# Four prompt-attention layers on one core: when a spare PSUM bank is handed back, how side tiles are spaced in the last layer's first chunk, and how the first weights arrive

## The chip, the cores and the metric

One core of a Trainium2 chip runs the whole kernel in one launch. The metric is the device time of one execution in microseconds. Before the change three runs took 2162.75, 2163.64 and 2164.74 us, median 2163.64. By about 0.2% (4.3 us) and less, two kernels of this length are treated here as equal.

## The reference

`x` is 2048 tokens by 640 features. Four attention layers are applied, each as `x = x + f(layernorm(x))`, in the order A, B, A, B. Both A and B have 32 heads of 20 features; A and B have their own `wqkv` (640 x 1920) and `wo` (640 x 640).

```
qkv = x @ wqkv                       # q, k, v: 32 heads of 20
scores = einsum("bhqd,bhkd->bhqk", q, k) * 20 ** -0.5
A: scores masked to 0 <= row - col < 256     # layers 0 and 2
B: all 2048 x 2048 scores, no mask           # layers 1 and 3
out = softmax(scores) @ v, then @ wo
```

The exponentials of layers 1 and 3 are 2 x 32 x 2048 x 2048 numbers. They decide which engine is busy longest.

## The kernel before, in words

**Tiles.** Scores are made transposed: 128 keys by 512 queries of one head is one *tile*, one PSUM bank. A *unit* (class `Unit`) is one group of four heads (`g`, 0 to 7) of one layer `l` and one chunk `c` of 512 queries. A unit of a full layer has 16 key blocks x 4 heads = 64 tiles; a windowed unit has 12. Layer 1's chunk 0 and layer 3's chunk 0 are cut by keys (`PARTS`): layer 3's chunk 0 into a part of 48 tiles (key blocks 0 to 11) and a part of 16 (blocks 12 to 15) per head group, since keys of the last chunk exist only after layer 2's last chunk.

**The loop.** The list `units` is the order of work; layers are interleaved. After layer 1's last chunk it holds: layer 3 chunk 0 part one for groups 0 to 3, the eight windowed units of layer 2 chunk 3, part one for groups 4 to 7, part two for groups 0 to 7, and then layer 3 chunks 1 to 3 (`index[3, 1, 0, None]` is where those begin). One pass of the main loop is a *tick*: score matmuls (L1427) of two or three tiles into one of two PSUM areas (banks 0 to 2, or 3 to 5 and 6), one exponential on ACT over all of them (L1453), and, a few ticks later, the four matmuls of a key block with the values (L1486) into bank 7.

**Side tiles.** Some tiles of layers 1 and 3 don't go to ACT. `side_giver` picks a loaded unit, `side_take` takes tiles from its end, and VectorE (DVE) makes the exponential: `side_fixed` (L1000) reads the scores out of PSUM, then for each pair of tiles a `chain` of four steps, `fraction` L1016, `square` L1024, `cubic` L1028 and `whole` L1034. In layer 1 a tile may be taken at the earliest `GAP_1` = 5 ticks after the one before and only while the planner's estimate of DVE's backlog, `state["lag"]`, is under `LAG_1` = 0.5; the steps `cubic` and `whole` are cut into two halves of 512 columns, and `side_work` fills DVE up to a backlog of `WORK_1` = 1.4. Once `side["late"]` is set, there is no gap, the limits are `LAG` = 0.95 and `WORK` = 2.2, and the steps are whole (1024 columns). `side_start` sets it when layer 3 chunk 0 part one reaches group 4 and no windowed unit holds `qa` or `ka`. Its buffers are two score buffers, one temporary in `spare`, where layer 2's weights were, and five output buffers in `ka_all` and `qa_all`.

**Background.** Projections (`project`), values (`t_v`), layer norm (`t_ln`), output projections (`t_out`, L600 is its DVE add) and the softmax tails (`t_tail`, `scaled`) are generators. `pump` advances them by the credit that `rate` gives out, so that a task is done some 16 ticks before the unit that needs it. `require` runs what is missing at once, when a unit can't wait. Each background block takes a PSUM bank with `take_m`, is read out by DVE (`evac`, L350, or L600, L1155, L1196) and gives the bank back with `drop_m`. After the interleaved start (`state["early"]` false) the only such bank is number 6: `drop_m` marks it free from the next tick on. TensorE's instructions stand in one queue, so a block that is issued before DVE has emptied bank 6 holds up all scores behind it. `keep_clock` adds dummy matmuls (masks by identity) where the planner finds TensorE too idle; on a tick in which bank 6 isn't free they go in front of the next tick's scores.

**The start.** The weights of layer 0 come on SyncE's queue (L136) into `raw`, a view of `spare`, as four transfers of 320 columns; `get_w` copies 80 columns at a time into padded tiles (POOL L363 zeroes, DVE L365 copies). `first_ln` normalises the first chunk at the same time.

Of the kernel before, what the change touches and what calls it, by code (L numbers as in the profile page):

```python
# [20 lines left out]
D = 640  # L21
# [3 lines left out]
KD = D // P  # L25
G = 8
C = 512
NC = S // C
EPS = 1e-5
SCALE = DH ** -0.5  # L30
HD = D // 2
# [7 lines left out]
KA = 18  # L39
LAG = 0.95  # L40
LAG_1 = 0.5
WORK = 2.2
WORK_1 = 1.4
# [1 line left out]
PRE_1 = 0.8  # L45
KEEP = 30
HALF = True
HALF_3 = False
MOST_1 = 64
GAP_1 = 5  # L50
QA = 4

PARTS = {
    l: [(e[n], e[n + 1]) for n in range(len(e) - 1)]
    for l, e in ((1, (0, 4, 8, 12, 16)), (3, (0, 12, 16)))
}
# [3 lines left out]
def kernel(  # L60
# [10 lines left out]
    nc = tc.nc  # L71
# [29 lines left out]
    spare = big.tile([P, 3 * KD * C], BF16, name="spare", tag="spare")  # L101
    raw = spare[:, 0 : KD * 2 * D].rearrange("p (c f) -> p c f", c=KD)
# [13 lines left out]
    ka_all = big.tile([P, KA, C], BF16, name="ka", tag="ka")  # L116
    kas = [ka_all[:, n, :] for n in range(KA)]
    qa_all = big.tile([P, QA, C], BF16, name="qa", tag="qa")
# [10 lines left out]
    wq_view = [w.rearrange("(c p) f -> p c f", p=P) for w in wqkv_in]  # L129
    nc.sync.dma_start(out=x_sb[:, 0:2, :], in_=xin[:, 0:2, :])  # L130
    nc.sync.dma_start(out=x_sb[:, 2:4, :], in_=xin[:, 2:4, :])

    for h in range(2):
        for n in range(2):
            a = n * D + h * HD
            nc.sync.dma_start(out=raw[:, :, a : a + HD], in_=wq_view[0][:, :, a : a + HD])  # L136
    nc.sync.dma_start(out=wv_sb[0][:], in_=wq_view[0][:, :, 2 * D : 3 * D])
    for c in range(1, NC):
        nc.sync.dma_start(out=x_sb[:, 4 * c : 4 * c + 4, :], in_=xin[:, 4 * c : 4 * c + 4, :])
# [6 lines left out]
    def load_wop(w, dense):  # L146
# [9 lines left out]
        out=ident[:], in_=ident[:], compare_op=ALU.not_equal, fill=1.0,  # L156
# [6 lines left out]
    for m, b, ge in (  # L163
# [6 lines left out]
            out=v, in_=v, compare_op=ALU.is_ge if ge else ALU.is_gt, fill=0.0,  # L170
# [29 lines left out]
    ready = set()  # L200
    todo = []
    tails = []
    state = {"tick": 0, "held": None, "credit": 0.0, "early": True, "act": True, "unit": 0, "heat": 0.0, "carry": 0.0, "least": 0.0, "floor": 0.0, "owed": 0, "lag": 0.0, "want": 0}
# [75 lines left out]
    mfree = {5: (0, 0), 6: (0, 1)}  # L279
    mseq = [1]  # L280
# [9 lines left out]

    def drop_m(b):
        mseq[0] += 1
        mfree[b] = (state["tick"] + (not state["early"]), mseq[0])

    def end_early():
        while mfree[5][0] == 1 << 30:
# [22 lines left out]
    live = Counter()  # L319
# [210 lines left out]
    ka = {}  # L530
    qa = {}
# [233 lines left out]
    early = deque(Unit(1, 0, g, p) for p in PARTS[1][:3] for g in range(G))  # L765
# [17 lines left out]
    index = {(u.l, u.c, u.g, u.part): n for n, u in enumerate(units)}  # L783
# [91 lines left out]
    def finish_unit(u):  # L875
# [33 lines left out]

    side_out = {}  # L910
    side = {
        "xi": deque(), "chain": deque(), "out": deque(), "late": False, "early": False,
        "half": None, "at": 0, "last": 0,
    }
    givers = [u for u in units if not u.windowed and (u.l, u.c) != (1, 0)]
# [1 line left out]
    def side_tiles(xi, t, outs):  # L917

        side["xi"].extend(xi)
        side["t"] = t  # L920
        side["out"].extend(outs)

    def side_start():

        assert not side["chain"] and side["half"] is None
        assert ("k", 2, NC - 1, KD - 1) in ready and ("q", 2, NC - 1, KD - 1) in ready
        f = [spare[:, n * 4 * C : (n + 1) * 4 * C].bitcast(F32) for n in range(2)]
        side["xi"].clear()
        side["out"].clear()
        outs = [ka_all[:, KA - 6 + 2 * n : KA - 4 + 2 * n, :] for n in range(3)]  # L930
        outs += [qa_all[:, 2 * n : 2 * n + 2, :] for n in range(2)]
        side_tiles(f[0:2], spare[:, 8 * C : 10 * C].bitcast(F16), outs)
        side["late"] = True

    def side_early():

        b = part_o["t"]
        f = [b[:, 2 * n : 2 * n + 2, :].rearrange("p a b -> p (a b)") for n in range(2)]
        outs = [b[:, n, :].bitcast(BF16).rearrange("p (a b) -> p a b", a=2) for n in range(5, G)]
        side_tiles(f, b[:, 4, :].bitcast(F16), outs)  # L940
        side["early"] = True

    def side_giver():

        if not side["late"] and state["tick"] < side["last"] + GAP_1:
            return None
        if side["half"] is not None:
            return side["half"][0]
        if not side["xi"]:
            return None  # L950
        while side["at"] < len(givers) and not givers[side["at"]].rest:
            side["at"] += 1
        for n in range(side["at"], min(side["at"] + 3, len(givers))):
            u = givers[n]
            if id(u) not in loaded or state["tick"] < loaded[id(u)] + 8:
                return None
            if not side["late" if u.l == 3 else "early"]:
                return None
            if u.l == 1 and len(u.aside) >= MOST_1:
                continue  # L960
            if len(u.rest) >= (KEEP if len(u.rest) + len(u.aside) < u.size else 12):
                side["at"] = n
                return u
        return None
# [43 lines left out]
    def chain(u, xi):  # L1008

        V = nc.vector  # L1010
        t = side["t"]
        low = xi.bitcast(I16)[:, 0::2]
        box = {}

        def fraction(h):
            V.tensor_scalar(  # L1016
                out=t[:, h], in0=low[:, h], scalar1=T1, scalar2=T0, op0=ALU.mult, op1=ALU.add
            )

        def square(h):  # L1020
            if "out" not in box:
                box["out"] = side["out"].popleft()
            q = box["q"] = box["out"].rearrange("p a b -> p (a b)").bitcast(F16)
            V.tensor_tensor(out=q[:, h], in0=t[:, h], in1=t[:, h], op=ALU.mult)  # L1024

        def cubic(h):
            q = box["q"]
            V.scalar_tensor_tensor(  # L1028
                out=q[:, h], in0=q[:, h], scalar=TB, in1=t[:, h], op0=ALU.add, op1=ALU.mult
            )  # L1030

        def whole(h):
            q = box["q"]
            V.scalar_tensor_tensor(  # L1034
                out=q.bitcast(U16)[:, h], in0=xi.bitcast(I32)[:, h], scalar=1.0 / C,
                in1=q[:, h], op0=ALU.mult, op1=ALU.add,
            )
            if h.stop == 2 * C:
                side["xi"].append(xi)
                side_out.setdefault(id(u), []).append((box["out"], state["tick"]))  # L1040

        every = (slice(0, 2 * C),)
        halves = (slice(0, C), slice(C, 2 * C)) if HALF and (u.l == 1 or HALF_3) else every
        cost = 0.7 if len(halves) == 2 else 1.25
        steps = [(fraction, h, 0.7) for h in every] + [(square, h, 0.7) for h in every]
        steps += [(cubic, h, cost) for h in halves] + [(whole, h, cost) for h in halves]
        return deque(steps)

    def side_work(force, limit=None):

        if limit is None:
            limit = WORK if side["late"] else WORK_1
        while side["chain"]:
            step, h, cost = side["chain"][0][0]
            if step.__name__ == "square" and not side["out"]:
                return False
            if not force and state["lag"] + cost > limit:
                return False
            side["chain"][0].popleft()
            if not side["chain"][0]:  # L1060
                side["chain"].popleft()
            step(h)
            state["lag"] += cost
            if force:
                return True
        return False
# [240 lines left out]
    with tc.manual_schedule():  # L1307
# [12 lines left out]
        n = 0.0  # L1320
# [61 lines left out]
        while ended is None or t < ended + 8:  # L1382
            t += 1
            state["tick"] += 1
            n_b = 0
            if flow:
                if not side["early"] and state["unit"] >= index[1, 1, 0, None]:
                    side_early()
                if (
                    not side["late"] and state["unit"] >= index[3, 0, 4, PARTS[3][0]]  # L1390
                    and not live["qa"] and not live["ka"]
                ):
                    side_start()
                if state["unit"] >= final:
                    last_tick[0] = 0
                giver = side_giver() if state["lag"] < (LAG if side["late"] else LAG_1) else None
                if giver is not None and state["unit"] >= final and (
                    state["held"] is not None or mfree[6][0] > state["tick"]
                    or state["want"] >= state["tick"] - 1
                ):  # L1400
                    giver = None
                cur = next_tile(t, giver)
                n_b = len(cur)
                for b in cur:
                    u = b[0]
# [42 lines left out]
                while i < n_b:  # L1448
                    b0 = cur[i][3]
                    k = i  # L1450
                    while k < n_b and cur[k][3] == b0:
                        k += 1
                    nc.scalar.activation(  # L1453
                        out=pt[:, i:k, b0 * P :], in_=sp[:, i:k, b0 * P :],
# [12 lines left out]
            for n in range(2 if n_b == 0 or t > closed + 1 else 0):  # L1467
                u = pts[0][3][0] if pts else None
# [10 lines left out]
                first, last = group[0][3][5:7]  # L1479
# [20 lines left out]
                    closed = t  # L1500
                    break

            if n_b and not side["late"]:
                side_work(False, PRE_1)
            if n_b and not state["early"]:
                background(t, n_b)
# [5 lines left out]
            if t > 0 and masked is not None:  # L1512
                cur_, pt_ = masked
                i = 0
                while i < len(cur_):
# [5 lines left out]
                    for b in ((3,), (1, 2), (0,))[m] if split else ():  # L1521
                        if b < b0:
# [4 lines left out]
                            out=v, in_=v, compare_op=ALU.is_gt if later else ALU.is_ge, fill=0.0,  # L1527
# [3 lines left out]
                    if split and m != 1:  # L1531
# [6 lines left out]
                            out=pt_[:, i:k, cols], in0=pt_[:, i:k, cols], in1=mv_, op=ALU.mult  # L1538
                        )
                    elif m is not None and not split:  # L1540
# [6 lines left out]
                            out=pt_[:, i:k, cols], in0=pt_[:, i:k, cols], in1=mv_, op=ALU.mult  # L1547
# [38 lines left out]
```

## Time and profile before

| | us |
|---|---|
| median of 3 runs | 2163.64 |
| profiled execution, its own time | 2161.81 |
| its span, first to last instruction | 2160.1 |
| ACT busy | 2085.4 (97%) |
| PE busy | 1925.8 (89%) |
| DVE busy | 1484.4 (69%) |
| POOL busy | 360.2 (17%) |
| mean granted TensorE clock | 0.997 |

Busy is the time in which an engine has an instruction under way. Line numbers such as L1453 are those of the kernel's listing. Tables by stretch give, for each stretch of the span in us, its length and then each engine's busy time and number of instructions, the granted TensorE clock, the DMA share and GB/s. Tables of waits give who waited for whom: engine, what it was about to write and its line, the releaser, and then total us, number of times and the longest.

### The profile page before, as it was taken

Reading aid. Unit: us, or ns where it says so; the run is one execution under the profiler, and the core shown is the slowest. Engines: PE = TensorE matmul, PEld = TensorE weight load, DVE = VectorE, ACT = ScalarE, POOL = GpSimd, SP = SyncE. Lnnn points to the kernel's source line nnn. Section 1 sums busy time; section 2 is a strip of 40 time slices with the busy share of each in tenths; the row PEclk is TensorE's granted clock in tenths of the full one; section 3 lists DMA queues with packets and bytes.
Section 4 is the critical chain, followed back from the end, with each engine's and each line's share of the span. In section 5 each row is a group of like instructions: output and inputs, shape, how many; then the busy total and the mean of one; then the engine's idle time right before and its main releaser. Section 6 shows DMA issues by size and latency. Waiting matters only on the chain. (4 is left out here: it accounts for less than half of the span.)

```text
span 2160.1 us, 73113 instructions
## 1 busy us (share of the span) xinstructions
PE 1925.8 (89%) x31774; PEld 755.2 (35%) x31775; DVE 1484.4 (69%) x2619; ACT 2085.4 (97%) x1717; POOL 360.2 (17%) x803
## 2 busy tenths in 40 slices
PE   8999999988888898888988989888898989888898
PEld 4444443433333333333333433332332222222222
DVE  6656665426666676776767733676678888987886
ACT  7899899999999999999999999989999999999997
POOL 6543434100021002400033001500000000000000
PEclk9999999999999999999999999999999999999999
DMA  6212222222210222111120112111121111111100
GB/s 205 64 57 73 57 58 68 73 59 59 59 47 19 63 53 71 36 31 47 50 86 23 38 55 75 33 45 50 53 60 44 35 36 42 32 33 41 44 25 17
DMA packets 80128, 114.33 MB, mean 53 GB/s; under 512 B 18398, under 2 KB 61758, under 8 KB 79806
## 3 DMA queue, kind: packets, MB, share of 16 engines
q1 hardware_dynamic: 70190, 81.06, 14.0%
q0 software_dynamic: 9616, 28.59, 3.8%
q8 instruction: 249, 4.08, 0.8%
q14 instruction: 73, 0.60, 0.1%
HBM read 76.58 MB, written 27.79 MB: 48 GB/s over the span
## 5 line engine op out<-in xcount | busy, mean ns | idle before, releaser
L1453 ACT ACTIVATE pt<-ps 128x1536 bf16<-128x1536 f32 (+2 forms) x1641 | 2051.5, 1412 | 41.7 <-PE ps L1427 31.6
L1427 PE MATMUL ps<-qt,kt 32*128 32x512 bf16 x3913 | 544.7, 384 | 59.4 <-ACT pt L1453 51.8
L317 PE MATMUL ps<-masks,ident 128*32 128x512 bf16 x5668 | 506.7, 384 | 95.8 <-ACT pt L1453 48.5
L1486 PE MATMUL ps<-pt,vt 128*21 128x512 bf16 x3776 | 376.4, 386 | 0.3 <-ACT pt L1453 0.2
L1427 PEld LDWEIGHTS <-kt 32*128 32x128 bf16 x3913 | 154.6, 91 | 457.8 <-issue 436.9
L317 PEld LDWEIGHTS <-ident 128*32 128x32 bf16 x5668 | 181.2, 94 | 282.0 <-issue 256.1
L1526 POOL TENSOR_SCALAR_AFFINE_SELECT pt<-pt 128x256 bf16<-128x256 bf16 (+2 forms) x506 | 217.9, 452 | 199.4 <-ACT pt L1453 186.5
L350 DVE CAST st<-ps 128x512 bf16<-128x512 f32 x134 | 92.6, 691 | 139.0 <-PE ps L317 138.7
L1486 PEld LDWEIGHTS <-vt 128*21 128x21 bf16 x3776 | 93.4, 89 | 257.7 <-issue 254.0
L317 PE MATMUL ps<-wop,on 128*32 128x320 bf16 x3712 | 160.6, 300 | 6.0 <-DVE x_sb L600 3.9
L1000 DVE TENSOR_SCALAR spare<-ps 128x512 int32<-128x512 f32 x208 | 142.8, 687 | 29.5 <-PE ps L982 23.1
L1537 DVE TENSOR_TENSOR pt<-pt,masks 128x256 bf16<-128x256 bf16 (+3 forms) x268 | 115.5, 447 | 45.4 <-ACT pt L1453 43.3
L317 PEld LDWEIGHTS <-on 128*32 128x32 bf16 x5760 | 122.2, 95 | 64.2 <-issue 30.4
L1427 PE MATMUL ps<-qa,ka 32*128 32x384 bf16 (+2 forms) x1408 | 118.1, 276 | 22.9 <-ACT pt L1453 19.8
L1196 DVE TENSOR_TENSOR on<-on,ps 128x512 bf16<-128x512 bf16 x128 | 86.5, 685 | 59.5 <-PE ps L317 57.2
L600 DVE TENSOR_TENSOR x_sb<-x_sb,ps 128x320 bf16<-128x320 bf16 x120 | 58.3, 486 | 99.5 <-PE ps L317 98.9
L317 PE MATMUL ps<-wv,xnT 128*32 128x320 bf16 x2560 | 117.1, 303 | 10.2 <-DVE on L1196 3.0
L317 PE MATMUL ps<-xnT,spare 128*32 128x512 bf16 x1720 | 118.2, 381 | 5.5 <-DVE on L1196 1.8
L317 PE MATMUL ps<-xnT,wqk 128*32 128x512 bf16 x1600 | 108.1, 381 | 6.7 <-DVE xnT L1301 1.3
L1000 DVE TENSOR_SCALAR raw_o<-ps 128x512 int32<-128x512 f32 x112 | 76.9, 686 | 47.5 <-PE ps L1427 46.7
L902 DVE CAST on<-ps 128x512 bf16<-128x512 f32 x112 | 76.8, 686 | 36.0 <-PE ps L1486 28.8
L568 POOL DMA_DIRECT2D k_d<-st x75 | 41.6, 555 | 270.0 <-DVE st L350 247.0
(99 smaller groups left out, 1744.2 us busy)
## 6 DMA issues: line engine op xcount, KB each, us to landing
vt<-v_d SPq DMA_DIRECT2D x48, 336.0 KB
kt<-k_d SPq DMA_DIRECT2D x192, 80.0 KB
k_d<-st POOLq DMA_DIRECT2D x75, 128.0 KB, 2.1
q_d<-st POOLq DMA_DIRECT2D x75, 128.0 KB, 2.1
qt<-q_d SPq DMA_DIRECT2D x384, 20.0 KB
v_d<-vs POOLq DMA_DIRECT2D x16, 336.0 KB, 3.0
qa<-q_d SPq DMA_DIRECT2D x224, 20.0 KB
ka<-k_d SPq DMA_DIRECT2D x224, 20.0 KB
```

The lines of the kernel that those rows point to most:

```text
L317: nc.tensor.matmul(out_[r], lhsT=lhsT[:, r], rhs=rhs, start=start, stop=stop)
L350: nc.vector.tensor_copy(out=out_, in_=in_)
L568: nc.gpsimd.dma_start(out=dst, in_=staging.pop())
L600: nc.vector.tensor_tensor(out=xv, in0=had, in1=yp, op=ALU.add)
L902: nc.vector.tensor_copy(out=oT, in_=op)
L1000: nc.vector.tensor_scalar(out=xi.bitcast(I32)[:, i * C : (i + 1) * C], in0=z, scalar1=SCALE * LOG2E * FIX, scalar2=127.5 * FIX, op0=ALU.mu ...
L1196: nc.vector.tensor_tensor(out=oT, in0=oT, in1=zb, op=ALU.mult)
L1427: nc.tensor.matmul(sp[:, i, col * P : (col + qn) * P], lhsT=u.k(kc, j), rhs=u.q(j, q0, qn), start=True, stop=True,)
L1453: nc.scalar.activation(out=pt[:, i:k, b0 * P :], in_=sp[:, i:k, b0 * P :], func=ACT.Exp, scale=SCALE,)
L1486: nc.tensor.matmul(op[32 * j : 32 * j + VW, q0 * P : (q0 + qn) * P], lhsT=u.v(kc, j), rhs=pg[:, i, col * P : (col + qn) * P], start=(first ...
L1526: nc.gpsimd.affine_select(out=v, in_=v, compare_op=ALU.is_gt if later else ALU.is_ge, fill=0.0, base=0, pattern=[[0, k - i], [-1 if later ...
L1537: nc.vector.tensor_tensor(out=pt_[:, i:k, cols], in0=pt_[:, i:k, cols], in1=mv_, op=ALU.mult)
```

## The change

- `drop_m`: with `state["early"]` false, the bank is free from the next tick on as before; if `state["lag"]` is over `SLOW` = 0.9 and the loop hasn't reached layer 3 chunk 1, from the tick after that.
- `freely()`, true from layer 3 chunk 1 on, takes the place of `side["late"]` where gap, limits, halves and order of DVE's work are chosen. Layer 3 chunk 0 so has the gap of 5 ticks, `LAG_1`, `WORK_1` and halved steps.
- `side_start` runs when layer 2 chunk 3 has been reached and its q and k are projected, with one output buffer in `spare`; the five others are added by `side_more` under the old condition.
- Units under 32 tiles (layer 3 chunk 0, part two) give no side tiles. `MOST_1`, a bound of 64 that no unit reached, is gone.
- The first weights come in six transfers, of 160, 160 and 320 columns for q and k each.

```diff
+SLOW = 0.9
-    for h in range(2):
+    for a0, a1 in ((0, 160), (160, HD), (HD, D)):
         for n in range(2):
-            a = n * D + h * HD
-            nc.sync.dma_start(out=raw[:, :, a : a + HD], in_=wq_view[0][:, :, a : a + HD])
+            a = slice(n * D + a0, n * D + a1)
+            nc.sync.dma_start(out=raw[:, :, a], in_=wq_view[0][:, :, a])
...
-        mfree[b] = (state["tick"] + (not state["early"]), mseq[0])
+        mfree[b] = (state["tick"] + (not state["early"]) * (1 + (state["lag"] > SLOW and state["unit"] < index[3, 1, 0, None])), mseq[0])
...
-        outs = [ka_all[:, KA - 6 + 2 * n : KA - 4 + 2 * n, :] for n in range(3)]
-        outs += [qa_all[:, 2 * n : 2 * n + 2, :] for n in range(2)]
+        outs = [spare[:, 10 * C : 12 * C].rearrange("p (a b) -> p a b", a=2)]
...
+    def side_more():
+
+        side["out"].extend(ka_all[:, KA - 6 + 2 * n : KA - 4 + 2 * n, :] for n in range(3))
+        side["out"].extend(qa_all[:, 2 * n : 2 * n + 2, :] for n in range(2))
+        side["more"] = True
...
+    def freely():
+
+        return state["unit"] >= index[3, 1, 0, None]
...
-        if not side["late"] and state["tick"] < side["last"] + GAP_1:
+        if not freely() and state["tick"] < side["last"] + GAP_1:
...
-            if u.l == 1 and len(u.aside) >= MOST_1:
+            if u.size < 32:
                 continue
...
-        halves = (slice(0, C), slice(C, 2 * C)) if HALF and (u.l == 1 or HALF_3) else every
+        halves = (slice(0, C), slice(C, 2 * C)) if HALF and not freely() else every
...
-            limit = WORK if side["late"] else WORK_1
+            limit = WORK if freely() else WORK_1
...
-                    not side["late"] and state["unit"] >= index[3, 0, 4, PARTS[3][0]]
-                    and not live["qa"] and not live["ka"]
+                    not side["late"] and state["unit"] >= index[2, NC - 1, 0, None]
+                    and all((n, 2, NC - 1, KD - 1) in ready for n in "qk")
                 ):
                     side_start()
+                if side["late"] and not side["more"] and not live["qa"] and not live["ka"] and state["unit"] >= index[3, 0, 4, PARTS[3][0]]:
+                    side_more()
...
-                giver = side_giver() if state["lag"] < (LAG if side["late"] else LAG_1) else None
+                giver = side_giver() if state["lag"] < (LAG if freely() else LAG_1) else None
...
-            if n_b and not side["late"]:
+            if n_b and not freely():
                 side_work(False, PRE_1)
```

More of the change, by code (lines that the diff above doesn't have):

```diff
@@ L47 @@
 HALF = True
-HALF_3 = False
-MOST_1 = 64
+SLOW = 0.9
 GAP_1 = 5
@@ L911 @@
     side = {
-        "xi": deque(), "chain": deque(), "out": deque(), "late": False, "early": False,
+        "xi": deque(), "chain": deque(), "out": deque(), "late": False, "early": False, "more": False,
         "half": None, "at": 0, "last": 0,
```

## The prediction

> **What bounds the kernel now.** The page's first part comes first, the busy shares:
>
> ```profile
> PE 1925.8 (89%) x31774; PEld 755.2 (35%) x31775; DVE 1484.4 (69%) x2619; ACT 2085.4 (97%) x1717; POOL 360.2 (17%) x803
> ```
>
> ACT is busy for all but 75 us of the 2160.1 us span. So the time changes in two ways only: ACT gets more or fewer tiles, or those gaps grow or shrink. The table by stretch says where the gaps lie (length; PE, PEld, DVE, ACT, POOL busy; clock, DMA share, GB/s):
>
> ```profile
> 440.00:1240.00 800.00, 709.53 (x11925) 289.05 (x11926) 540.51 (x1036) 794.12 (x643) 129.05 (x267) 1.00 0.18 49
> 1240.00:1392.00 152.00, 132.90 (x2290) 54.53 (x2283) 63.72 (x135) 151.85 (x114) 39.51 (x86) 1.00 0.21 59
> 1392.00:1531.00 139.00, 119.82 (x1912) 47.05 (x1915) 92.09 (x149) 129.02 (x102) 10.61 (x20) 0.99 0.17 46
> 1531.00:2132.00 601.00, 539.38 (x7216) 167.90 (x7215) 516.12 (x681) 598.37 (x445) 0.00 (x0) 1.00 0.14 38
> ```
>
> The four rows are layer 1 with spaced side tiles, a stretch without side tiles, layer 3 chunk 0 with unspaced ones, and layer 3 chunks 1 to 3. ACT's idle share is 0.74%, 0.10%, 7.2% and 0.44%. The second row has the same kinds of background blocks as the others, so blocks alone stop nobody; the third row loses 139.00 - 129.02 = 9.98 us. The waits of that stretch say to whom:
>
> ```profile
> ACT pt L1453 <- PE ps L1427: 8.9, 16, 1.3
> PE ps L317 <- DVE st L350: 3.7, 6, 1.4
> PE ps L317 <- DVE x_sb L600: 2.8, 4, 1.3
> PE ps L317 <- DVE vs L350: 2.4, 4, 1.2
> ```
>
> ACT waits for scores, and TensorE's block matmuls (L317) wait for DVE to empty bank 6. The timeline shows one case in order of time (start, duration, engine, line; idle before and releaser in brackets):
>
> ```profile
> 1404.69 1.22 DVE L1034 SCALAR_TENSOR_TENSOR ka<-spare,ka 128x1024 uint16<-128x1024 int32 x1
> 1404.82 1.27 PE L317 MATMUL ps<-wop,on 128*32 128x320 bf16 x32
> ...
> 1406.65 0.48 DVE L600 TENSOR_TENSOR x_sb<-x_sb,ps 128x320 bf16<-128x320 bf16 x1
> ...
> 1407.18 1.27 PE L317 MATMUL ps<-wop,on 128*32 128x320 bf16 x32 [0.76 <-DVE x_sb L600]
> 1408.38 0.39 PE L1427 MATMUL ps<-qt,kt 32*128 32x512 bf16 x3
> ...
> 1408.88 1.45 ACT L1453 ACTIVATE pt<-ps 128x1536 bf16<-128x1536 f32 x1 [1.34 <-PE ps L1427]
> ```
>
> A whole side step of 1.22 us stands ahead of the add L600; the next block waits 0.76 us for the bank, the scores stand behind that block, and ACT idles 1.34 us.
>
> **The change part by part.**
>
> *Gap, limits and halves in layer 3 chunk 0.* The stretch 1392 to 1531 gets the regime of layer 1. At layer 1's 0.74% it would idle 1.0 us; layer 1's worst 40 us window, 1200 to 1240, has 1.30 us (38.70 busy), and at that rate the 92 us with side tiles would idle 3.0. I take 2.0, so 8.0 us are gained; the ends are a gain of 9 and, if spacing cures only half, of 4. What is late next is the score matmul behind ACT itself, as in layer 1 (PE L1427 for ACT: 41.7 us there). Halved steps cost DVE 2 x (688 + 685) - (1219 + 1220) = 307 ns a pair, 2.5 us over some 8 pairs; they lie in DVE's 47 us of idle time in the stretch and cost nothing, at worst 2.5 us if that room isn't where they fall.
>
> *Fewer side tiles.* Now L1000 runs 20 times from 1392 to 1484 and twice to 1531. Layer 1 made 112 from 490 to 1245, one per 6.74 us. After the change the part-one units last about 80 us, of which the last 5 or so give none (12 tiles must be left in the unit), so 75 / 6.74 = 11. The early start adds those taken beside the windowed units: layer 2's last projection is read out at 1353.1 and the first part-one unit after them starts at 1392, 38 us or 5.6 tiles, and two score buffers with one output buffer allow three pairs at most; I take 5. So 16 instead of 22. A tile more on ACT costs the difference of the two forms of L1453, 1529 - 1076 = 453 ns: 6 tiles are 2.7 us, on the path since ACT is the bound. Ends: 2 tiles (0.9) and 14 tiles (6.3), if the tighter limit of 0.5 keeps most of them out. The two tiles of part two are in this count; with them goes a pair that made the value matmuls of the first part-two units late (DVE L900 waited 2.9 us for PE L1076).
>
> *Side work beside the windowed units.* From 1347 to 1392 ACT is busy 45.00 of 45 us and DVE 24.4. Layer 1's windowed stretch 600 to 640, which had side tiles, idled 0.56 us. I take a loss of 0.5, ends 0 and 1.5.
>
> *The bank a tick later.* It acts from 440 to 1531 (before that there are two spare banks and the old rule). From 440 to 1240 PE waits 27.8 us, 74 times, for DVE to empty the bank, and ACT 4.1 us for scores. A block that comes a tick later finds the bank empty. I take half, 2.0 us gained; the upper end is all 4.1. What queues behind the later bank is every other block, tails included; what that costs at worst is the slower rival below. Dummy matmuls move ahead of the scores of the next tick; a group of four takes TensorE about 0.22 us, and PE waits 41.7 us for ACT in these 800 us, which covers them.
>
> *The first weights.* SyncE issues six transfers instead of four (0.47 to 0.95 us each, now 1.81 to 4.6), so those of `wv` and of the other x chunks are issued about 1.3 us later. The cover is traffic already queued: DMA runs at 362 to 396 GB/s from 7 to 12 us, long after the issues. What the weights release is the first copy L365. No wait for them is shown: DVE starts it at 9.82, straight behind the copy before it. It then takes 2495 ns where the median of that line is 348, while POOL writes its memsets from 9.26 to 12.18 without a gap. If that is POOL's doing, pieces bring nothing; if it hides a wait for weights, up to 2.1 us. I take 0, with ends of a gain of 2.1 and a loss of 1.3, since the copy's long duration ends with POOL's.
>
> The Trainium skill speaks on both sides here. "SBUF — State Buffer", section "Who interferes with whom", says that VectorE and GpSimd share a port pair under an exclusive lock, the loser blocking fully; the row agrees, and by it the term is 0. "Perfetto Trace Analysis", section "DMA Optimizations", says that splitting a transfer may let work start sooner; by that alone the sum would be up to 2 us lower.
>
> **Sum.** -8.0 + 2.7 + 0.5 - 2.0 + 0 = -6.8 us. The profiled execution took 2161.81 us, 1.8 under the median of the runs, so 2155.0 in its terms and 2157 as a median.
>
> **The rivals.**
>
> *Wash.* The stall shrinks by half only (4 us) and the limit of 0.5 keeps 14 tiles out (6.3 us), with 0.5 more beside the windows and the bank's 2.0 gained: -4.0 + 6.3 + 0.5 - 2.0 = +0.8, 2164. For it: DVE's load per us is higher in 1392 to 1484 than in layer 1. Against it: layer 1's 1160 to 1200 has DVE busy 31.7 of 40 us, and ACT loses 0.12 us there; it is the unhalved, bunched steps that differ.
>
> *Slower: projections come late.* Bank 6 is the only spare one. Each block that is read under a backlog pushes the next one back up to a tick (1.33 us). If q, k or values aren't there when a unit starts, `require` issues them in a row with no scores between: a projection block's 16 matmuls take 1.05 us, its read 0.69, so four in a row less the 1.33 us that ACT still has cost 5.6 us. There are five such deadlines (layer 2's four chunks, layer 3's part two); missing three by four blocks costs 17, which with the -6.8 gives 2174. It decides from two missed deadlines on. Against it: the last projection before the windows is read at 1353.1 and needed by group 6 at about 1347.7 + 6 x 5.4 = 1380, 27 us or 20 ticks; a deadline has about 30 blocks, so some 20 of them would have to be pushed. DVE was late in 74 of some 280 reads of the bank from 440 to 1240 (54 st, 48 x_sb, 72 va, vs and xnT, 53 on, 53 of the tails' small ones), a quarter. For it: in the trace of before the planner's backlog can't be seen, and every read adds 0.5 to 0.8 to it ahead of the test at 0.9.
>
> The Trainium skill's "Perfetto Trace Analysis", section "Matmul Optimizations", asks to keep all eight PSUM banks in use, which speaks for this rival; no row of before shows what holding the bank costs.
>
> *More than forecast.* All of ACT's 4.1 us and the 2.1 us of the first copy are won: 2157 - 2.1 - 2.1 = 2153.
>
> *It doesn't do what it says.* The early start may yield one pair, the rest waiting for an output buffer: 3 tiles fewer, 1.4 us, 2158; a part of the forecast's own range.
>
> **How the numbers follow.** Forecast with its variants, 2151 to 2159: 0.64, of which 0.06 below 2150. Wash, 2159.3 to 2168: 0.20. Late projections, above 2168 from two missed deadlines on (-6.8 + 11.2 = +4.4): 0.16. The range 2150 to 2171, which takes in two missed deadlines, leaves out 0.06 below and 0.13 above. Faster by over 0.2% (below 2159.3) 0.64; within 0.2% 0.18; slower, above 2168, 0.18 (the late projections and the wash's worst).
>
> **What would show it.** Right: ACT idle under 3 us in the 139 us from the first part-one unit after the windows; PE's waits for DVE st, x_sb and vs there from 8.9 to about 3; L1000 first at about 1355 and 14 to 18 times before layer 3 chunk 1; halved L1028 and L1034 forms there; PE's waits for DVE from 440 to 1240 near 14 us; the first L317 matmul still at about 13.0 us. Wrong: rows of L317 in bursts of two or more blocks between scores at the start of windowed units; under 10 side tiles; ACT still waiting over 5 us for scores in that stretch; or a first copy that ends before 11 us.

## The result and the profile after

Five runs of the changed kernel took 2182.17 to 2186.55 us, median 2184.43; the kernel before, in runs beside them, 2164.42. The ratio is 1.0093, with a 95% interval of 1.0082 to 1.0103: slower by 20 us, above the forecast range. The profiled execution took 2182.17 us, its span is 2180.5. In the listing after, the lines named so far are: exponential L1463 (before L1453), scores L1437 (L1427), block matmuls L316 (L317), eviction L349 (L350), the add L599 (L600), side tiles L1008 (L1000), values L1496 (L1486).

The busy shares of the changed kernel:

```profile
PE 1939.7 (89%) x32014; PEld 754.8 (35%) x32015; DVE 1473.3 (68%) x2623; ACT 2090.6 (96%) x1718; POOL 362.6 (17%) x807
```

ACT has 5.2 us more work and 89.9 instead of 74.7 us of idle time. The table by stretch of the changed kernel (length; PE, PEld, DVE, ACT, POOL busy; clock, DMA share, GB/s) says where:

```profile
440.00:1240.00 800.00, 707.33 (x11818) 281.44 (x11821) 533.91 (x1023) 786.37 (x637) 125.76 (x263) 1.00 0.18 47
1240.00:1374.00 134.00, 116.02 (x1886) 47.12 (x1882) 52.23 (x102) 121.25 (x91) 14.35 (x28) 0.97 0.22 62
1374.00:1414.00 40.00, 34.29 (x736) 14.68 (x729) 30.64 (x65) 40.00 (x32) 28.76 (x64) 1.00 0.19 51
1414.00:1553.00 139.00, 120.09 (x1980) 48.28 (x1980) 75.39 (x144) 135.77 (x105) 12.30 (x22) 1.00 0.18 48
1553.00:2154.00 601.00, 538.40 (x7184) 166.72 (x7180) 511.80 (x675) 597.21 (x444) 0.00 (x0) 1.00 0.13 38
```

The fourth row is layer 3 chunk 0 after the windowed units: ACT idles 3.2 us there instead of 9.98, as the change meant. The loss is ahead of it. From 440 to 1240 ACT idles 13.6 us (5.9 before), and from 1240 to 1374, where before it idled 0.15 us in 152, it idles 12.75, at a granted clock of 0.97. The waits of the changed kernel from 440 to 1240:

```profile
PE ps L316 <- ACT pt L1463: 59.8, 147, 1.4
...
PE ps L1437 <- ACT pt L1463: 20.7, 64, 0.6
...
ACT pt L1463 <- PE ps L1437: 9.8, 30, 0.9
...
PE ps L316 <- DVE st L349: 1.8, 5, 0.5
...
PE ps L316 <- DVE x_sb L599: 1.4, 5, 0.3
```

TensorE's waits for DVE have all but gone, from 27.8 us to about 5. But TensorE now waits 80.5 us for ACT (51.2 before), and ACT waits for scores more than twice as long, 9.8 us instead of 4.1. L316 (L317 before) is a helper's line that background blocks and dummy matmuls share, and the view by tile keeps them apart. For `ident`, which is in every dummy matmul, the kernel before has from 440 to 1240:

```profile
L317 PE MATMUL ps<-masks,ident x1900: 376/379/392, 447.9 to 1222.8; 128*32 128x512 bf16 x190
...
  ACT pt L1453: 9.5, 30
  DVE st L350: 7.7, 18
  DVE on L1196: 4.1, 9
  DVE x_sb L600: 3.7, 14
...
```

With four smaller rows for DVE that aren't shown, 20.7 of the 27.8 us and 54 of the 74 waits for DVE were those of dummies, not of blocks. In the changed kernel the same view has all 147 waits and 59.8 us of L316 for ACT: they are the dummies' too.

To place the time, the end of each unit (the last DVE read of its value sums) is matched in both traces. The stretch between two such ends, before and after, in us:

| up to the end of | before | after | difference |
|---|---|---|---|
| layer 1 chunk 1, groups 0 to 3 | 109.12 | 111.67 | +2.55 |
| ... groups 4 to 7, with windowed units | 143.08 | 142.72 | -0.36 |
| layer 1 chunk 2, groups 0 to 3 | 109.34 | 109.60 | +0.26 |
| ... groups 4 to 7 | 150.10 | 154.47 | +4.37 |
| layer 1 chunk 3, groups 0 to 3 | 108.05 | 109.98 | +1.93 |
| ... groups 4 to 7 | 153.51 | 162.94 | +9.43 |
| layer 3 chunk 0 part one, groups 0 to 3 | 86.29 | 90.95 | +4.66 |
| windowed units, layer 2 chunk 3 | 45.06 | 43.88 | -1.18 |
| part one, groups 4 to 7 | 87.28 | 82.73 | -4.55 |
| part two | 59.32 | 58.36 | -0.96 |
| layer 3 chunk 1 | 203.39 | 206.58 | +3.19 |

22.8 us are lost by the time part one's group 3 ends, 14.1 of them in two lumps (+9.43 and +4.66); 6.7 are won in chunk 0; 3.2 are lost again in chunk 1. ACT's idle time in the same stretches grew by 6.5 us up to the first lump, and by 9.5 and 4.3 us in the two. The first lump in the timeline of the changed kernel (start, duration, engine, line; idle before and releaser in brackets):

```profile
1270.47 1.26 PE L316 MATMUL ps<-xnT,wqk 128*32 128x512 bf16 x20
...
1271.78 0.69 DVE L349 CAST st<-ps 128x512 bf16<-128x512 f32 x1 [1.36 <-PE ps L316]
...
1272.76 0.55 POOL L567 DMA_DIRECT2D k_d<-st  x1 [1.05 <-DVE st L349]
...
1275.84 0.28 SPq L825 DMA_DIRECT2D kt<-k_d  x1
...
1277.88 0.60 PE L1437 MATMUL ps<-qt,kt 32*128 32x512 bf16 x1 [5.83 <-DMA kt<-k_d]
...
1278.58 1.45 ACT L1463 ACTIVATE pt<-ps 128x1536 bf16<-128x1536 f32 x1 [6.83 <-PE ps L1437]
...
1281.43 2.90 ACT L1463 ACTIVATE pt<-ps 128x1536 bf16<-128x1536 f32 x2 [1.40 <-PE ps L1437]
```

A key projection for layer 3 is issued only when its unit starts. Its copy ends at 1272.47; the keys go out to memory, are fetched back, and the first scores run at 1277.88, 5.4 us later. ACT idles 6.83 and then 1.40 us. The second lump is milder: background blocks stand in front of the scores tick after tick.

```profile
1357.38 1.45 ACT L1463 ACTIVATE pt<-ps 128x1536 bf16<-128x1536 f32 x1 [0.26 <-PE ps L1437]
1357.74 1.26 PE L316 MATMUL ps<-xnT,spare 128*32 128x512 bf16 x20 [0.47 <-DVE st L349]
...
1359.43 1.45 ACT L1463 ACTIVATE pt<-ps 128x1536 bf16<-128x1536 f32 x1 [0.61 <-PE ps L1437]
1359.79 1.26 PE L316 MATMUL ps<-xnT,spare 128*32 128x512 bf16 x20
...
1361.48 2.79 ACT L1463 ACTIVATE pt<-ps 128x1536 bf16<-128x1536 f32 x2 [0.60 <-PE ps L1437]
```

The 20 matmuls of one projection block, 1.26 us, stand ahead of each tick's scores, and such a tick costs ACT up to 0.6 us.

### The profile page after: what moved, and what is told of

It is laid out like the page before. It is cut to its first block, busy times and chain, and to the rows that moved or that the text cites. A ratio compares the mean times of both kernels' runs of the same rounds, so it can differ in the third digit from the quotient of the medians.

```text
span 2180.5 us, 73602 instructions
## 1 busy us (share of the span) xinstructions
PE 1939.7 (89%) x32014; PEld 754.8 (35%) x32015; DVE 1473.3 (68%) x2623; ACT 2090.6 (96%) x1718; POOL 362.6 (17%) x807
## 5 line engine op out<-in xcount | busy, mean ns | idle before, releaser
L1463 ACT ACTIVATE pt<-ps 128x1536 bf16<-128x1536 f32 (+2 forms) x1642 | 2056.5, 1392 | 57.4 <-PE ps L1437 48.2
L316 PE MATMUL ps<-masks,ident 128*32 128x512 bf16 x5908 | 526.7, 385 | 137.3 <-ACT pt L1463 115.4
L1437 PE MATMUL ps<-qt,kt 32*128 32x512 bf16 x3913 | 544.5, 384 | 45.0 <-ACT pt L1463 33.8
L1496 PE MATMUL ps<-pt,vt 128*21 128x512 bf16 x3782 | 377.2, 386 | 0.4 <-ACT pt L1463 0.2
L316 PEld LDWEIGHTS <-ident 128*32 128x32 bf16 x5908 | 189.7, 94 | 339.9 <-issue 316.6
L1437 PEld LDWEIGHTS <-kt 32*128 32x128 bf16 x3913 | 146.5, 91 | 449.7 <-issue 429.9
L349 DVE CAST st<-ps 128x512 bf16<-128x512 f32 x134 | 92.6, 691 | 151.8 <-PE ps L316 151.3
L1496 PEld LDWEIGHTS <-vt 128*21 128x21 bf16 x3782 | 93.7, 89 | 253.5 <-issue 249.7
L316 PE MATMUL ps<-wop,on 128*32 128x320 bf16 x3712 | 158.8, 300 | 1.7 <-DVE x_sb L599 0.8
L1008 DVE TENSOR_SCALAR spare<-ps 128x512 int32<-128x512 f32 x200 | 137.2, 686 | 27.0 <-PE ps L990 22.6
L316 PEld LDWEIGHTS <-on 128*32 128x32 bf16 x5760 | 122.3, 95 | 55.2 <-issue 21.1
L1547 DVE TENSOR_TENSOR pt<-pt,masks 128x512 bf16<-128x512 bf16 (+3 forms) x272 | 117.8, 451 | 26.9 <-ACT pt L1463 24.9
L599 DVE TENSOR_TENSOR x_sb<-x_sb,ps 128x320 bf16<-128x320 bf16 x120 | 58.3, 486 | 106.8 <-PE ps L316 105.9
L1437 PE MATMUL ps<-qa,ka 32*128 32x384 bf16 (+2 forms) x1408 | 118.2, 277 | 13.8 <-ACT pt L1463 11.1
L316 PE MATMUL ps<-xnT,spare 128*32 128x512 bf16 x1720 | 113.9, 380 | 6.0 <-DVE on L1204 1.8
L316 PE MATMUL ps<-wv,xnT 128*32 128x320 bf16 x2560 | 111.8, 300 | 4.9 <-DVE on L1204 2.7
L316 PE MATMUL ps<-xnT,wqk 128*32 128x512 bf16 x1600 | 107.5, 385 | 4.1 <-DVE st L349 1.4
L1008 DVE TENSOR_SCALAR raw_o<-ps 128x512 int32<-128x512 f32 x114 | 78.3, 687 | 43.6 <-PE ps L1437 42.1
```

The costliest lines, as they stand in the source:

```text
L316: nc.tensor.matmul(out_[r], lhsT=lhsT[:, r], rhs=rhs, start=start, stop=stop)
L349: nc.vector.tensor_copy(out=out_, in_=in_)
L599: nc.vector.tensor_tensor(out=xv, in0=had, in1=yp, op=ALU.add)
L1008: nc.vector.tensor_scalar(out=xi.bitcast(I32)[:, i * C : (i + 1) * C], in0=z, scalar1=SCALE * LOG2E * FIX, scalar2=127.5 * FIX, op0=ALU.mu ...
L1437: nc.tensor.matmul(sp[:, i, col * P : (col + qn) * P], lhsT=u.k(kc, j), rhs=u.q(j, q0, qn), start=True, stop=True,)
L1463: nc.scalar.activation(out=pt[:, i:k, b0 * P :], in_=sp[:, i:k, b0 * P :], func=ACT.Exp, scale=SCALE,)
```

## The experiments

The theory: a block that finds the bank withheld is put off; put-off blocks are a debt, covered as long as the planner has ticks to spare, and paid in lumps at the unit that needs them. The rivals: the dummy matmuls that the rule also moves ahead of the scores; a loss that is the same for each late hand-over; and a combination of the parts.

**e1: the bank at the next tick again.** The rest of the change stays.

```diff
-        mfree[b] = (state["tick"] + (not state["early"]) * (1 + (state["lag"] > SLOW and state["unit"] < index[3, 1, 0, None])), mseq[0])
+        mfree[b] = (state["tick"] + (not state["early"]), mseq[0])
```

> The changed kernel with one line undone: bank 6 is free from the next tick on, whatever the backlog. Theory bank (the later hand-over costs all of the loss, spacing gains a little): between the landmarks of the two traces layers 1 and 2 lost 22.8 us, layer 3 chunk 0 gained 6.7 and layer 3 chunk 1 lost 3.2, so this takes 2184.4 - 22.8 = 2161.6, and ACT idles under 7 us from 440 to 1240. Rival spacing (spaced or fewer side tiles cost it): stays within 3 us of 2184.

2161.58 us, ratio 0.9990 (0.9981 to 1.0000). The stretches up to part one's group 3 are those of before to within some 0.02 us. So the whole loss hangs on that one line.

**e2: the late bank alone.** The kernel before with the edit of e1 turned round and nothing else.

> The kernel before with that one line added, and nothing else. Theory bank: 2164.4 + 22.8 = 2187, with a wait of TensorE for a key transfer of over 4 us near 1270. Rival combination (the later bank hurts only together with the earlier side start or the spacing): 2160 to 2168.

2181.28 us, ratio 1.0083 (1.0068 to 1.0099). Its stretches up to part one's group 3 are the changed kernel's within 0.2 us. It comes out below the expectation because the late bank also smooths layer 3 chunk 0 by itself: part one's groups 4 to 7 take 83.06 us in it, against 87.28 before, and ACT idles 3.2 us there instead of 8.3. There the late bank and the spacing cure the same stall.

**e3: blocks late, dummies by the old rule.**

```diff
+    extra = {}
...
-            if mfree[b][0] <= state["tick"]:
+            if mfree[b][0] + extra.get(b, 0) <= state["tick"]:
...
+        mfree[b] = (state["tick"] + (not state["early"]), mseq[0])
+        extra[b] = (not state["early"]) * (state["lag"] > SLOW and state["unit"] < index[3, 1, 0, None])
```

> The changed kernel in which blocks still get the bank a tick later, but the dummy matmuls are placed by the old rule (in bank 6 from the next tick on), so fewer of them stand in front of scores: 779 instead of 1087 by the planner's count. Theory dummies: the scattered part of the loss goes, 8.7 us up to layer 1 chunk 3 group 3, so 2175 or less, and TensorE's L316 waits for ACT fall from 59.8 us to about 10 in 440 to 1240. Theory late blocks: the 14.1 us in two lumps between 1264 and 1375 stay, and 2184 if they and the blocks' own delays are all.

2186.07 us, ratio 1.0102 (1.0084 to 1.0121). The waits from 440 to 1240 in e3, where the lines are L318, L1465 and L1439:

```profile
PE ps L318 <- ACT pt L1465: 20.1, 57, 0.8
...
ACT pt L1465 <- PE ps L1439: 10.4, 29, 0.8
```

The place of the dummies explains most of TensorE's new wait for ACT (59.8 us down to 20.1) and none of the time: ACT waits for scores as long as in the changed kernel. By tile, the dummies wait some 21 us for DVE again, as before the change, and that costs nothing either. The dummies are cleared, and TensorE's waits for DVE in layer 1, most of which are theirs, aren't what the time hangs on.

**e7: the late bank until layer 1 chunk 3 starts.**

The line of e1 again, cut to the term that differs:

```diff
-state["unit"] < index[3, 1, 0, None]
+state["unit"] < index[1, 3, 0, None]
```

> The changed kernel, but the bank is given back late only until layer 1 chunk 3 starts; from there on at the next tick again. Theory A (postponed blocks run up a debt that is paid in lumps where the blocks are due at last, at the end of layer 1 chunk 3 and in layer 3 chunk 0 part one): the lumps of 9.4 and 4.7 us go, and so does the small one in chunk 3's first half, 1.9; what was lost by then, some 6.7 us, stays: about 2168. Theory B (each late hand-over costs its own share at its own place, spread evenly): about 55% of the late hand-overs remain, and of 22.8 us some 12.5 stay: about 2174. Rival C (the backlog of blocks carries over into chunk 3 whatever the rule is there): the lumps stay, 2180 or more.

2169.61 us, ratio 1.0023 (1.0014 to 1.0033), as the theory of debt had it. Layer 1 chunk 3 and part one's groups 0 to 3 take 107.32, 153.89 and 86.28 us, those of before to within 0.8. The lumps are gone, and what was lost before chunk 3 stays lost: a debt isn't carried across the start of a chunk whose blocks are let go at once.

**e8: a bound of 1.5 in place of 0.9. e9: every hand-over late (a bound of -1).** By the planner's own count, about 80 and 390 late hand-overs against 258 in the changed kernel.

> The changed kernel with the bound for a late hand-over at 1.5 instead of 0.9, so that about 80 of 391 hand-overs are late instead of 258. Theory A (the deadlines have slack, and only a debt beyond it costs): nearly no loss is left, 2160 to 2164. Theory B (each late hand-over costs the same): 22.8 x 80 / 258 = 7 us are left, about 2168.5.

> The changed kernel with every hand-over before layer 3 chunk 1 late (391 instead of 258). Theory A (debt beyond the slack): more deadlines are missed, among them the projections of layer 2 chunk 2, and the loss grows faster than the number: over 2200, with a lump of 5 us or more at the end of layer 1 chunk 2. Theory B: 22.8 x 391 / 258 = 34.6 us of loss, about 2196, spread evenly.

e8: 2163.61 us, ratio 0.9997 (0.9988 to 1.0006). e9: 2223.07 us, ratio 1.0268 (1.0251 to 1.0285). The kernel before took 2163.9 to 2164.4 beside each of them. With e1, runs with 0, 80, 258 and 390 late hand-overs take 2161.6, 2163.6, 2184.4 and 2223.1 us: 0.025 us for each of the first 80 (2.0 us in all, which the intervals of e1 and e8 don't tell from nothing), 0.12 for each of the next 178, 0.29 for each of the rest. A fixed price per hand-over falls; a debt beyond a slack stands. The counts alone leave one doubt, since e8's hand-overs are those with the longest backlog and may be cheap for that reason; what speaks for the debt is e7 and where the lumps lie. When the planners of these kernels are run, `require` finds nothing missing after the interleaved start in the kernel before, in e7 and in e8. It finds one thing missing in the changed kernel, keys of chunk 2 for layer 3, and three in e9, the first of them queries of layer 2 chunk 2 that stand behind other blocks: nine are issued in a row.

The expectation had named the projections of layer 2 chunk 2, and rightly; the place it gave, the end of layer 1 chunk 2, was wrong (1.8 us in groups 4 to 7). e9 loses 22.2 us at the end of layer 1 chunk 3's groups 0 to 3, where layer 2 chunk 2's first windowed unit was to start, and 31.8 in the groups after. The timeline of e9 there:

```profile
1116.90 1.45 ACT L1463 ACTIVATE pt<-ps 128x1536 bf16<-128x1536 f32 x1 [0.16 <-PE ps L1437]
1117.07 0.86 PE L316 MATMUL ps<-wv,xnT 128*32 128x320 bf16 x20
...
1118.53 0.86 PE L316 MATMUL ps<-wv,xnT 128*32 128x320 bf16 x20 [0.59 <-DVE va L349]
...
1127.27 1.26 PE L316 MATMUL ps<-xnT,spare 128*32 128x512 bf16 x20 [0.59 <-DVE va L349]
...
1129.32 1.26 PE L316 MATMUL ps<-xnT,spare 128*32 128x512 bf16 x20 [0.79 <-DVE st L349]
...
1135.49 0.98 PE L1437 MATMUL ps<-qa,ka 32*128 32x128 bf16 x3 [4.37 <-DMA qa<-q_d]
...
1136.35 1.45 ACT L1463 ACTIVATE pt<-ps 128x1536 bf16<-128x1536 f32 x1 [18.00 <-PE ps L1437]
```

Value and projection blocks run in a row, each with its 0.59 or 0.79 us wait for DVE to empty the one bank, then the trip through memory; ACT idles 18.00 us in one piece. The table by stretch of e9 shows the granted clock after it (the third column from the end):

```profile
1110.00:1130.00 20.00, 13.88 (x286) 7.39 (x287) 10.01 (x18) 8.19 (x7) 0.43 (x1) 1.00 0.01 2
1130.00:1150.00 20.00, 10.86 (x154) 3.98 (x150) 5.77 (x11) 5.80 (x4) 3.15 (x7) 0.70 0.24 72
1150.00:1170.00 20.00, 14.22 (x189) 4.60 (x179) 7.66 (x15) 11.12 (x8) 9.45 (x23) 0.78 0.14 41
1170.00:1190.00 20.00, 18.48 (x242) 6.25 (x245) 10.68 (x21) 14.38 (x11) 5.03 (x11) 0.66 0.12 34
```

**e5: spacing alone.** The kernel before with `freely()` in the five places of the diff; no late bank, no pieces, no early start, part two gives tiles as before.

> The kernel before with gap, limits and halved steps of layer 1 for layer 3 chunk 0, and nothing else (side start, bank and weights as before). 314 side tiles instead of 320 by the planner. Theory: the 10 us of ACT idle in that stretch go to about 2, 6 tiles cost 2.7: 2164.4 - 8.0 + 2.7 = 2159. Rival wash (fewer tiles cost what the stall gave): 2163 to 2166.

2159.50 us, ratio 0.9979 (0.9969 to 0.9988). It is the fastest kernel here, ahead of the kernel before by 0.2%, which is about the size that counts as equal. Its table by stretch:

```profile
440.00:1240.00 800.00, 709.20 (x11917) 288.90 (x11916) 538.71 (x1034) 794.23 (x643) 129.38 (x267) 1.00 0.17 49
...
1393.00:1532.00 139.00, 122.54 (x1960) 48.62 (x1952) 85.09 (x157) 134.54 (x106) 11.73 (x22) 1.00 0.17 46
```

ACT idles 4.5 us in the stretch of 139 where it idled 9.98. e1, which adds the early start, the rule for small units and the pieces to this, isn't faster.

**e11: part two's units give side tiles again** (e1 without the rule for units under 32 tiles). **e12: e5 without a gap from part two on** (`index[3, 0, 0, PARTS[3][1]]` in `freely`). Both ask what chunk 1's 3.2 us are.

> The changed kernel with the bank given back at the next tick, and with the units of layer 3 chunk 0 part two giving side tiles again (5 of them, planned, instead of none). If the missing tiles there are the 2 to 3 us that layer 3 chunk 1 lost, the time from the end of part one to the end of chunk 1 falls from 264.2 us to 261.5 or less and the kernel is near 2159.5. If part two's stalls of before come back (1.6 us of ACT's idle time), it stays at 2161.6.

> The kernel before with spacing, lower limits and halves in layer 3 chunk 0 part one only, and no gap from part two on (8 side tiles planned there instead of 6). If DVE's tiles are all that counts there, 2 x 453 ns less than with the spacing in all of chunk 0: 2158.6. If the bunched tiles of part two stall TensorE as they did before, 1 us more: 2160.5.

e11: 2162.65 us, ratio 0.9993 (0.9984 to 1.0002). e12: 2160.20, ratio 0.9983 (0.9974 to 0.9991). In e11 chunk 1 takes 204.26 us instead of e1's 206.18, but part two takes 61.15 instead of 57.98. The tiles taken early do shorten chunk 1, and cost more than that where they are taken: ACT idles 2.13 us in part two (e1 none). So the time that chunk 1 lost for want of them is a trade and not a loss; the first of e11's two expectations fell. e12 has the same 2.1 us in part two, its intervals overlap with e5's, and nothing is won over e5.

**e6: the pieces alone. e10: e5 with two of POOL's clearing writes on VectorE.**

```diff
-        nc.gpsimd.memset(spread8[:], 0.0)
-        nc.gpsimd.memset(rts[:], 0.0)
+        nc.vector.memset(spread8[:], 0.0)
+        nc.vector.memset(rts[:], 0.0)
```

> The kernel before with the first weights in six transfers and nothing else. Step 5 of the prediction (pieces bring nothing): 2164, with the first L317 matmul between 11.9 and 13.0, as it falls out in the kernels with four transfers too. Rival (the copy waits for weights): the first L317 at 11.9 or earlier and 1 to 2 us faster, 2162 to 2163. The other side (later transfers come late): up to 1.3 us slower.

> The kernel before with the spacing part of the change alone, and two of the three clearing writes of the start (spread8 and rts) made by VectorE instead of GpSimd. If the first weight copy is long because GpSimd writes at the same time, GpSimd is done some 2 us earlier, the copy ends by about 11 instead of 12.4, and the first L318 block matmul starts by 12.0 instead of 13.0: about 2158.5. If the copy waits for the weights, that matmul stays at 13.0 and the time at 2159.5. If VectorE's extra work lies ahead of the first layer norm, up to 1 us is lost: 2160.5.

e6: 2164.83 us, ratio 1.0007 (0.9998 to 1.0016), the first block matmul at 13.31. e10: 2160.47, ratio 0.9983 (0.9973 to 0.9992), at 12.05. The starts in the timelines of e5 and then of e10:

```profile
10.20 2.24 DVE L365 COPY wqk<-spare 128x400 bf16<-128x400 bf16 x2
...
11.88 0.25 POOL L492 MEMSET va<- 128x32 bf16 x1
...
12.98 1.26 PE L317 MATMUL ps<-xnT,wqk 128*32 128x512 bf16 x20 [0.72 <-DVE xnT L1305]
```

```profile
9.21 1.69 POOL L363 MEMSET wqk<- 128x240 bf16 x6
...
9.86 0.61 DVE L365 COPY wqk<-spare 128x400 bf16<-128x400 bf16 x2
...
12.05 2.32 PE L317 MATMUL ps<-xnT,wqk 128*32 128x512 bf16 x37
```

In e5 the first of the two copies ends at 12.26, 0.14 us after POOL's last clearing write; in e10 it takes 0.27 us. In all 13 profiles the copy starts between 9.8 and 10.9. In nine it ends within 0.15 us of the end of POOL's last write, at 12.2 to 12.6; in four (the changed kernel, e7, e9, e10) it gets through at once. Pieces are on both sides (e6 and e8 blocked, e7 and e9 not), and so is a start as early as 9.83 (e12 blocked, e10 at 9.86 not). That clears the weights. e10 doesn't prove its own point, though: its copy passes while POOL is still at L363, ahead of the place of the writes that were moved. What decides who goes first stays open, and the microsecond at the start isn't seen in the total.

## Why the prediction was wrong

**The step that failed is "The bank a tick later": forecast a gain of 2.0 us, ends a gain of 4.1 and the slower rival.** The runs put it at a loss of some 18 to 22 us (e2 alone, 0.0083 of 2164.18; the changed kernel against e1, 1.0093 against 0.9990). Its first half was right: a bank handed back later is found empty, and PE's waits for DVE fell below the 14 us that the prediction named. But those waits weren't on the path: 20.7 of the 27.8 us were those of dummy matmuls, which the planner adds where it finds TensorE too idle. TensorE waited for ACT in their place, and ACT gained nothing. The prediction read all 27.8 us as waits of blocks, because the line of the helper, L317, is the same.

The rival *Slower: projections come late* is what happened, at a chance of 0.16 and a price of 2174. Three points of its dismissal failed:

- **"a quarter".** That share was read from TensorE's waits for DVE in the trace, dummies included. The rule doesn't ask DVE; it asks the planner's backlog, to which each read adds its 0.5 to 0.8 just ahead of the test. By the planner's own count 258 of 391 hand-overs were late, 66%. The prediction had this in the rival's "for it" and gave it no number. With 0.66 instead of 0.25, a deadline with 30 blocks loses 20 ticks, just the 20 that it had worked out as the slack.
- **"five such deadlines".** The list has layer 2's four chunks and layer 3's part two. The worst lump is at a sixth: the keys of chunk 2 for layer 3, due when part one starts (`kt`, 1277.88).
- **"5.6 us" for four blocks.** Blocks do run in a row with no scores between, as e9 shows. But a projection block is 20 matmuls in 1.26 us and not 16 in 1.05, and with its read and the waits the next one starts 2.05 us later, not 1.74 (1127.27 to 1129.32 in e9). The trip through memory was left out: 5.4 us from copy to scores in the changed kernel, 4.2 in e9 (1131.32 to 1135.49). And blocks that come in time but crammed cost 0.6 us a tick, which the price per missed deadline leaves out too.

**Gap, limits and halves.** Forecast -8.0 with ends of 9 and 4. ACT's idle time in the stretch of 139 us fell by 5.5 us in e5, and by 6.8 in the changed kernel, where the late bank helps (e2). 2.0 was too little to leave: in e5 2.2 us of waits for scores and 2.0 for the values' matmuls remain. Right in kind, somewhat over-sized.

**Fewer side tiles.** Forecast 22 to 16, +2.7. Before, L1000 ran 27 times up to the end of part two at 1542.8; the prediction stopped its count at 1531, with 22. The changed kernel has 18 up to the same end: nine fewer, 4.1 us at 453 ns. Five beside the windows and eleven in part one are as forecast; the term was short by the tiles after 1531. Over the whole kernel it is 314 against 320. e11 shows that having such tiles in part two is no cheaper.

**Side work beside the windowed units.** Forecast +0.5 of idle time; ACT idles nothing there (40.00 of 40 us busy from 1374 to 1414), so the term was 0, and small either way. That the stretch got 1.2 us shorter belongs to the five side tiles, which are counted above.

**The first weights.** Forecast 0; e6 gives 1.0007 (0.9998 to 1.0016). Right. The "wrong" sign that the prediction named, a first copy ending before 11 us, did come up in the changed kernel (10.28), by the race above and not by the pieces.

**The sum without the bank** is -4.8 us; e1 measured -2.2 (-4.1 to 0.0) and e5 -4.5 (-6.7 to -2.6). So everything but the one step would have stood within the range.

**What stays open.** Of the 22.8 us, 8.7 lie scattered ahead of the lumps. In e7, whose late rule ends where layer 1 chunk 3 starts, 6.3 us are lost by then, and 6.0 of them remain at the end of part one's group 3. They are many small interruptions: up to the first lump's stretch, gaps over 0.1 us between exponentials went from 14 to 32 and ACT's idle time from 4.0 to 10.5 us. Each costs a little more than its idle time, since two exponentials of 128x1536 in a row take 2.79 us (at 1361.48 above) and a lone one 1.45, so that an unbroken run needs about 1.34 for each. By that estimate 18 more interruptions cost some 2 us beside the 6.5 of idle time, which comes to about the 8.7. Which block is late in each of them wasn't followed up.

## What to carry to other kernels

A wait that isn't on the path is not a gain when removed: ask first whose wait it is, here mostly that of dummy matmuls on a helper's line, then which engine it delays, and how much of the bound engine's own idle time it ends. When a rule holds back a shared buffer, count how often its own test is true, in the terms of the test and not of the trace (a planner that runs ahead of the launch can be counted without the chip), and hold that against the slack of every consumer's deadline, the trip through memory included; the price is near nothing up to the slack and climbs steeply behind it (0.025, 0.12, 0.29 us per hand-over here). And a bundle of edits should be taken apart: the part that gains here gains 0.2% alone.

## What the runs showed of the hardware

**A gap on TensorE slows the matmuls behind it.** In the changed kernel the 20 matmuls of a projection block take 1.26 us ahead of the gap of 5.83 us (1270.47) and 2.32 behind it. The granted clock is 0.50 behind the gap (third column from the end of the second row):

```profile
1278.41 2.32 PE L316 MATMUL ps<-xnT,wqk 128*32 128x512 bf16 x20
...
1278.00:1283.00 5.00, 5.00 (x39) 1.18 (x42) 0.69 (x1) 3.02 (x3) 0.56 (x1) 0.50 0.46 134
```

In e9, with more gaps, the clock was 0.66 to 0.78 over three stretches of 20 us. So a late projection is paid for a second time in the blocks that are to catch up. The Trainium skill, "TensorE: Matmul & The Clock Gate", section "What's actually happening", says that the clock is halved behind an idle window of about 3.4 us. The trace agrees: within these two blocks a group of four matmuls starts 0.21 to 0.22 us after the one before it ahead of the gap, and 0.40 to 0.43 behind it. One record by itself lengthens less, from 0.39 to 0.60 us for scores over 512 queries.

**The trip out to memory and back** took 3.08 us from the issue of `k_d` to that of `kt` and 2.04 from there to the scores. The Trainium skill, "SBUF — State Buffer", section "The DMA setup-cost knee (why "@ 1 MiB" ≠ asymptote)", gives a roughly fixed 2 us for a transfer; the trace is at that for the second leg and above it for the first.

**VectorE's copy and POOL's clearing writes** shut each other out, but not in one way only: nine times the copy waited for up to seven writes in a row, and four times the two took turns, POOL's 0.30 us write then taking 0.38 to 0.41. The Trainium skill, "SBUF — State Buffer", section "Who interferes with whom", has the one that issues first hold the shared ports for its whole instruction, the other fully blocked; here, in the nine, that lasted until the queue of writes was empty.
